# Second stage of a delta-rule and expert kernel: three buffers for the output copies, the last pair in halves, its remainder and one copy on VectorE

## The chip, the cores and the metric

One core of a Trainium2 chip. The metric is device time in microseconds (us); less is better. Engines: TensorE (PE, with its weight loads as PEld), VectorE (DVE), ScalarE (ACT), GpSimd (POOL), SyncE (SP, which issues the DMAs).

## The reference, cut to what matters

A delta-rule recurrence gives 3072 tokens of 384 features; these go through two feed-forward layers of width 2048. The change lies in the second one and in the copies at the end of the first.

```python
x = ...              # delta rule, (3072, 384)
h = x @ w_in         # first layer, 384 -> 2048
g = where(h > 0, h, exp(min(h, 0)) - 1)
x = g @ w_out        # 2048 -> 384
h = x @ w_in2        # second layer
P = a0 + a1*h + a2*h*h + a3*h*h*h
Q = 1 + abs(b0)*abs(h) + abs(b1)*h*h
out = (P / (Q + 1e-6)) @ w_out2
```

## The kernel before, in words

Everything is float32; each product of two float32 matrices is made of three matmuls, from a high part (type fp32r) and a remainder of either operand: high x high, high x remainder, remainder x high.

Tokens stand in the free dimension, features in partitions. The first stage works in windows of 512 tokens (the delta rule interleaved with the first layer); `evac1` (L623) copies a window's three accumulators `o0` to `o2` from PSUM to SBUF on ScalarE (`xe`) and sends them to DRAM (`x2d`). In the last window the copies go to the tiles `ys`, which the second stage uses as well.

The second stage (L639 to L725) works in six blocks of 512 tokens (`g`) and, in each, in eight pairs (`j`) of 128 hidden rows; pairs are numbered through, k = 8 g + j, 0 to 47. The steps of a pair:

- `H2`: 18 matmuls (L577 to L579, via `h_mms`) give 128 x 2 x 512 hidden values in PSUM, in `h_b` and `h_a` by turns.
- `A2`: three activations on ScalarE, 128x1024 each: square, absolute value and a linear form (L683, L684, L685) into `sq`, `ab`, `u`, which lie in the old tile `wo1` (named `wo` in the profile).
- `B2`: VectorE sums Q (L691); ScalarE takes its logarithm and the exponential of minus that, so 1/Q (L692, L693); VectorE makes the polynomial (L694 and L695, which read the PSUM values once more).
- `C2`: VectorE makes the high part `gh` (L702) and the error of it (L703, L704); POOL multiplies that into the remainder `gl` (L705).
- `O2`: 18 output matmuls (L719) add to the three accumulators, 12 with `gh` and then 6 with `gl`.

At the end of a block `evac2` (L722) copies the accumulators on ScalarE to tiles `ys` and sends each to DRAM. The pool `p2q` has two buffers for a tile name, so a third `ys` waits for the DMA of the first. The three accumulators have one PSUM bank each, and the next block's first matmul on a bank waits for its copy. The two-buffer rule holds for `h` too: `H2` of pair k + 2 comes before `O2` of pair k.

The order of the work is written by hand: `at(t, fn)` (L739) puts a step at a time t of a schedule, the list is sorted (L872), and each engine gets its instructions in that order; up to t = P + 4, the first two pairs of the second stage, the framework's scheduler reorders them (L877), after that they stand as listed. The lines that matter:

```python
at(t, H2, k)            # t = P + 2 * k
at(t + 1.05, A2, k)
at(t + 1.5, B2, k)
at(t + 2.2, C2, k)
at(t + 5.0, O2, k)
...
at(P + 16 * g + 19.9 + .1 * c, evac2, g, c)
```

So on ScalarE the copies of a block stand behind `B2` of pair 8 g + 9 and ahead of `A2` of pair 8 g + 10. POOL also makes the remainder of the next block's input (`lo_x2`, L664), in five places of a block.

Of the kernel before, what the change touches and what calls it, by code (L numbers as in the profile page):

```python
# [7 lines left out]
F32 = mybir.dt.float32  # L8
# [14 lines left out]
WINS = [[s, s + 1] for s in range(0, NSC, 2)]  # L23
NG2 = NT // 512
SLOTS = [[0, 0, 1, 3, 5, 7, 8, 9, 10, 11], [13, 15, 16, 18, 20, 22, 23, 26, 25, 27]]
HD = DM // 2
# [10 lines left out]
def kernel(  # L37
# [585 lines left out]
    def evac1(w):  # L623
        NC = 256 * len(WINS[w])
        c0 = 256 * WINS[w][0]
        for c in range(3):
            if w == NW - 1:
                xs = p2q.tile([128, 512], F32, tag="ys", name="xe")[:, 0:NC]
            elif c < 2:
                xs = ap2.tile([128, 8, 2, D], F32, tag="ub", name="xe").rearrange("p a b c -> p (a b c)")[:, 0:NC]  # L630
            else:
                xs = tmp[:, 0:NC]
# [44 lines left out]

    def A2(k):
        ps = flat(hp[k])
        w = wo1.rearrange("p f n -> p (f n)")  # L680
        sq, ab, u = (w[:, 1024 * (2 * i + k % 2):1024 * (2 * i + k % 2) + 1024] for i in range(3))
        e2[k] = sq, ab, u
        act(out=sq, in_=ps, func=AF.Square, scale=rb_sb)  # L683
        act(out=ab, in_=ps, func=AF.Abs, scale=ab_sb[:, 4:5])  # L684
        act(out=u, in_=ps, func=AF.Identity, scale=ab_sb[:, 3:4], bias=ab_sb[:, 2:3])  # L685

    def B2(k):
        ps = flat(hp.pop(k))
        sq, ab, u = e2[k]
        v = nc.vector  # L690
# [5 lines left out]

    def C2(k):
        sq, ab, u = e2.pop(k)
        v = nc.vector
        gh = p2q.tile([128, 1024], F32R, tag="gh2", name="gh2")  # L700
        gl = p2q.tile([128, 1024], F32R, tag="gl2", name="gl2")
        v.scalar_tensor_tensor(out=gh, in0=u, scalar=ab_sb[:, 0:1], in1=ab, op0=ALU.add, op1=ALU.mult)  # L702
        v.tensor_tensor(out=sq, in0=sq, in1=gh.bitcast(F32), op=ALU.mult)  # L703
        v.scalar_tensor_tensor(out=sq, in0=u, scalar=ab_sb[:, 0:1], in1=sq, op0=ALU.add, op1=ALU.subtract)  # L704
        nc.gpsimd.tensor_tensor(out=gl, in0=sq, in1=ab, op=ALU.mult)  # L705
        gt[k] = gh, gl

# [14 lines left out]
    def evac2(g, c):  # L722
        ys = p2q.tile([128, 512], F32, tag="ys", name="ys")
        act(out=ys, in_=acc["b", g][c], func=AF.Copy)  # L724
        nc.sync.dma_start(out=out[:, c, 512 * g:512 * g + 512], in_=ys)  # L725
# [130 lines left out]
    for k in range(NP * NG2):  # L856
        t = P + 2 * k
        at(t, H2, k)
        at(t + 1.05, A2, k)
        at(t + 1.5, B2, k)  # L860
# [110 lines left out]
```

## Time and profile before

| what | value |
|---|---|
| time, median of 3 runs | 1142.12 us (1136.59 to 1148.31) |
| the profiled execution's own time | 1144.03 us |
| its span, first to last instruction | 1142.2 us |
| TensorE matmul busy | 1046.1 us, 92% of the span |
| VectorE busy | 903.3 us, 79% |
| ScalarE busy | 772.3 us, 68% |
| POOL busy | 464.1 us, 41% |
| mean granted TensorE clock | 0.947 of full |

The first stage and the delta rule take about 735 us, the second stage the rest. All times below are from the span's start. In a row of a timeline the columns are start, length, engine, line, operation, tiles written and read, shape and count; in brackets the engine's idle time before it and what ended it. Matmuls are pipelined, so twelve matmuls of 0.39 us stand as one row of 2.88 us. A busy share is an average over stages with different limits; the waits between the engines say which one counts where.

### The profile page before, as it was taken

What the parts mean: (1) busy time and instruction counts of PE and PEld (TensorE: products, weight loads), DVE (VectorE), ACT (ScalarE), POOL (GpSimd) and SP (SyncE); (2) the same over time, 40 slices, a digit from 0 to 9 for tenths busy, and PEclk for the clock granted to TensorE, in tenths of its full rate; (3) what the DMA queues carried; (4) which work ended last, traced back from release to release, by engine and by line L of the source; (5) the groups of instructions that cost most, each with busy time, mean ns of one, the idle gap of its engine ahead of it and who ended that gap; (6) DMA issues with size and microseconds to landing.
All of it is one profiled execution on the core that took longest, in us unless ns stands there. A gap on an engine that the chain in (4) does not pass through costs nothing.

```text
span 1142.2 us, 20625 instructions
## 1 busy us (share of the span) xinstructions
PE 1046.1 (92%) x7952; PEld 836.8 (73%) x7952; DVE 903.3 (79%) x1231; ACT 772.3 (68%) x1521; POOL 464.1 (41%) x400
## 2 busy tenths in 40 slices
PE   7179898889798999999999999999999999999997
PEld 6055676667686778777878878778787887878885
DVE  4986979779856873795434479999999999999996
ACT  4566687776576646666565699976766767656764
POOL 1484466424332323243322245455353544535432
PEclk9567889999998999999999999999999999999999
DMA  9534444363364213120221054300101001010000
GB/s 262 175 123 129 120 137 131 109 207 110 100 185 145 62 61 121 56 79 2 79 71 38 1 170 127 116 10 1 56 1 56 1 1 56 1 56 1 28 1 28
DMA packets 51842, 91.75 MB, mean 80 GB/s; under 512 B 7072, under 2 KB 29728, under 8 KB 51744
## 3 DMA queue, kind: packets, MB, share of 16 engines
q1 hardware_dynamic: 51744, 90.43, 25.4%
q8 instruction: 62, 1.02, 0.4%
q14 instruction: 36, 0.29, 0.1%
HBM read 77.83 MB, written 12.58 MB: 79 GB/s over the span
## 4 chain that ended last, share of the span: by engine, by line
PE 53%; DVE 26%; ACT 7%; issue 7%; DMA 4%; POOL 4%; SPq 0%; POOLq 0%; DVEq 0%; ACTq 0%
PE o L719 12%; PE h_a L577 6%; PE h_a L578 5%; PE h_a L579 5%; DVE tmp L344 5%; PE o L595 3%; PE o L596 3%; PE o L597 3%; PE gp L278 2%; DVE tt L345 2%; PE h_b L577 2%; PE h_b L578 2%; PE h_b L579 2%; DVE wo L691 2%; DVE e L612 1%
## 5 line engine op out<-in xcount | busy, mean ns | idle before, releaser
L705 POOL TENSOR_TENSOR gl<-wo 128x1024 fp32r<-128x1024 f32 x48 | 146.4, 3051 | 215.2 <-DVE wo L704 183.1
L71 POOL TENSOR_TENSOR wor<-wo,wor 128x384 fp32r<-128x384 f32 x96 | 108.8, 1135 | 264.8 <-ACT wor L70 257.2
L577 PE MATMUL h_a<-xh,wi 128*128 128x512 f32 x417 | 174.2, 418 | 11.1 <-ACT pe L607 11.0
L578 PE MATMUL h_a<-xl,wi 128*128 128x512 f32 x417 | 169.8, 407 | 3.8 <-DVE xl L396 3.8
L579 PE MATMUL h_a<-xh,wi 128*128 128x512 f32 x417 | 168.2, 403 | 0.0
L719 PE MATMUL o<-gh,wo 128*128 128x512 f32 x576 | 141.9, 394 | 6.4 <-ACT ys L724 6.4
L719 PEld LDWEIGHTS o<-gh,wo 128*128 128x128 f32 x576 | 107.8, 189 | 33.0 <-ACT ys L724 10.8
L612 DVE SCALAR_TENSOR_TENSOR e<-e,pe 128x512 f32<-128x512 f32 x96 | 69.3, 722 | 76.0 <-ACT e L608 75.7
L595 PE MATMUL o<-gh,wor 128*128 128x512 f32 x288 | 116.4, 412 | 0.0
L596 PE MATMUL o<-gl,wor 128*128 128x512 f32 x288 | 114.4, 397 | 1.2 <-DVE gl L620 1.2
L597 PE MATMUL o<-gh,wor 128*128 128x512 f32 x288 | 113.2, 393 | 0.0
L577 PEld LDWEIGHTS h_a<-xh,wi 128*128 128x128 f32 x417 | 80.8, 194 | 31.6 <-ACT pe L607 13.7
L620 DVE TENSOR_TENSOR gl<-e,gh 128x512 fp32r<-128x512 f32 x88 | 77.4, 880 | 29.0 <-ACT gh L618 28.6
L578 PEld LDWEIGHTS h_a<-xl,wi 128*128 128x128 f32 x417 | 81.5, 195 | 22.7 <-DVE xl L396 7.8
L692 ACT ACTIVATE wo<-wo 128x1024 f32<-128x1024 f32 x48 | 51.0, 1063 | 64.8 <-DVE wo L691 64.8
L606 ACT ACTIVATE e<-h_a 128x512 f32<-128x512 f32 x91 | 54.3, 596 | 59.2 <-PE h_a L579 58.8
L579 PEld LDWEIGHTS h_a<-xh,wi 128*128 128x128 f32 x417 | 81.4, 195 | 17.3
L618 ACT ACTIVATE gh<-e 128x512 fp32r<-128x512 f32 x96 | 60.1, 626 | 33.7 <-DVE e L612 33.7
L691 DVE SCALAR_TENSOR_TENSOR wo<-wo 128x1024 f32<-128x1024 f32 x48 | 75.6, 1575 | 8.7 <-ACT wo L684 8.6
L719 PE MATMUL o<-gl,wo 128*128 128x512 f32 x288 | 73.8, 392 | 3.4 <-POOL gl L705 3.4
L70 ACT ACTIVATE wor<-wo 128x384 fp32r<-128x384 f32 x96 | 50.3, 524 | 36.2 <-PE o L597 35.3
L702 DVE SCALAR_TENSOR_TENSOR gh<-wo,ab_sb 128x1024 fp32r<-128x1024 f32 x48 | 65.3, 1359 | 8.1 <-ACT wo L693 2.0
(162 smaller groups left out, 2456.0 us busy)
## 6 DMA issues: line engine op xcount, KB each, us to landing
kv<-c_kv SPq DMA_DIRECT2D x24, 576.0 KB, 4.2
gin<-g_in SPq DMA_DIRECT2D x69, 192.0 KB, 2.7
kq<-c_kq SPq DMA_DIRECT2D x22, 512.0 KB, 4.0
raw<-w_out SPq DMA_DIRECT2D x42, 192.0 KB, 2.5
raw<-w_in SPq DMA_DIRECT2D x34, 192.0 KB, 2.4
wo<-w_in SPq DMA_DIRECT2D x30, 192.0 KB, 2.8
xr<-x2d SPq DMA_DIRECT2D x6, 768.0 KB, 5.8
out_t<-ys SPq DMA_DIRECT2D x18, 256.0 KB, 2.1
```

The costliest lines, as they stand in the source:

```text
L71: eng.tensor_tensor(out=t[:, 1], in0=src, in1=t[:, 0].bitcast(F32), op=ALU.subtract)
L577: mm(out=ps, lhsT=hi, rhs=xh[:, c, 0:NC], start=(c == 0), stop=False)
L578: mm(out=ps, lhsT=hi, rhs=xl[:, c, 0:NC], start=False, stop=False)
L579: mm(out=ps, lhsT=lo, rhs=xh[:, c, 0:NC], start=False, stop=(c == 2))
L595: mm(out=ps[:, 0:NC], lhsT=hi[:, cs], rhs=gh[:, 0:NC], start=(f == 0), stop=False)
L596: mm(out=ps[:, 0:NC], lhsT=hi[:, cs], rhs=gl[:, 0:NC], start=False, stop=False)
L597: mm(out=ps[:, 0:NC], lhsT=lo[:, cs], rhs=gh[:, 0:NC], start=False, stop=(f == NF - 1))
L612: nc.vector.scalar_tensor_tensor(out=e, in0=e, scalar=-1.0, in1=p, op0=ALU.add, op1=ALU.add)
L620: eng.tensor_tensor(out=gl[:, 0:NC], in0=e, in1=gh[:, 0:NC].bitcast(F32), op=ALU.subtract)
L691: v.scalar_tensor_tensor(out=sq, in0=sq, scalar=1.0 + 1e-6, in1=ab, op0=ALU.add, op1=ALU.add)
L705: nc.gpsimd.tensor_tensor(out=gl, in0=sq, in1=ab, op=ALU.mult)
L719: mm(out=ps, lhsT=wo2[2 * j + i][:, int(p == 1), cs], rhs=(gl if p == 2 else gh)[:, n], start=(j == 0 and p == 0 and i == 0), stop=(j == N ...
```

## The change

Four edits. `ys` gets three buffers, for the second stage and for the last window of the first. The last pair, k = 47 (`NK - 1`), runs `A2`, `B2` and `C2` twice, on 512 columns each (one of the two hidden row tiles), with its remainder `gl` on VectorE instead of POOL. Its output matmuls are ordered by half (`O2last`): nine for the first hidden tile, then nine for the second, with `gl` last in each. And of the last block's three output copies the middle one goes to VectorE.

```diff
--- before.py
+++ after.py
@@ -22,6 +22,7 @@
 NT = 3072
 WINS = [[s, s + 1] for s in range(0, NSC, 2)]
 NG2 = NT // 512
+NK = NF // 2 * NG2
 SLOTS = [[0, 0, 1, 3, 5, 7, 8, 9, 10, 11], [13, 15, 16, 18, 20, 22, 23, 26, 25, 27]]
 HD = DM // 2
 NV = 15
@@ -625,7 +626,7 @@
         c0 = 256 * WINS[w][0]
         for c in range(3):
             if w == NW - 1:
-                xs = p2q.tile([128, 512], F32, tag="ys", name="xe")[:, 0:NC]
+                xs = p2q.tile([128, 512], F32, tag="ys", name="xe", bufs=3)[:, 0:NC]
             elif c < 2:
                 xs = ap2.tile([128, 8, 2, D], F32, tag="ub", name="xe").rearrange("p a b c -> p (a b c)")[:, 0:NC]
             else:
@@ -675,18 +676,21 @@
     def flat(t):
         return t.rearrange("p a b -> p (a b)")
 
-    def A2(k):
+    ALL = slice(0, 1024)
+
+    def A2(k, n=ALL):
         ps = flat(hp[k])
         w = wo1.rearrange("p f n -> p (f n)")
-        sq, ab, u = (w[:, 1024 * (2 * i + k % 2):1024 * (2 * i + k % 2) + 1024] for i in range(3))
-        e2[k] = sq, ab, u
-        act(out=sq, in_=ps, func=AF.Square, scale=rb_sb)
-        act(out=ab, in_=ps, func=AF.Abs, scale=ab_sb[:, 4:5])
-        act(out=u, in_=ps, func=AF.Identity, scale=ab_sb[:, 3:4], bias=ab_sb[:, 2:3])
-
-    def B2(k):
-        ps = flat(hp.pop(k))
-        sq, ab, u = e2[k]
+        if k not in e2:
+            e2[k] = [w[:, 1024 * (2 * i + k % 2):1024 * (2 * i + k % 2) + 1024] for i in range(3)]
+        sq, ab, u = (t[:, n] for t in e2[k])
+        act(out=sq, in_=ps[:, n], func=AF.Square, scale=rb_sb)
+        act(out=ab, in_=ps[:, n], func=AF.Abs, scale=ab_sb[:, 4:5])
+        act(out=u, in_=ps[:, n], func=AF.Identity, scale=ab_sb[:, 3:4], bias=ab_sb[:, 2:3])
+
+    def B2(k, n=ALL):
+        ps = flat(hp[k])[:, n]
+        sq, ab, u = (t[:, n] for t in e2[k])
         v = nc.vector
         v.scalar_tensor_tensor(out=sq, in0=sq, scalar=1.0 + 1e-6, in1=ab, op0=ALU.add, op1=ALU.add)
         act(out=ab, in_=sq, func=AF.Ln)
@@ -694,16 +698,26 @@
         v.tensor_tensor(out=u, in0=u, in1=ps, op=ALU.mult)
         v.scalar_tensor_tensor(out=u, in0=u, scalar=ab_sb[:, 1:2], in1=ps, op0=ALU.add, op1=ALU.mult)
 
-    def C2(k):
-        sq, ab, u = e2.pop(k)
+    def C2(k, n=ALL):
+        sq, ab, u = (t[:, n] for t in e2[k])
         v = nc.vector
-        gh = p2q.tile([128, 1024], F32R, tag="gh2", name="gh2")
-        gl = p2q.tile([128, 1024], F32R, tag="gl2", name="gl2")
+        if k not in gt:
+            gt[k] = tuple(p2q.tile([128, 1024], F32R, tag=t, name=t) for t in ("gh2", "gl2"))
+        gh, gl = (t[:, n] for t in gt[k])
         v.scalar_tensor_tensor(out=gh, in0=u, scalar=ab_sb[:, 0:1], in1=ab, op0=ALU.add, op1=ALU.mult)
         v.tensor_tensor(out=sq, in0=sq, in1=gh.bitcast(F32), op=ALU.mult)
         v.scalar_tensor_tensor(out=sq, in0=u, scalar=ab_sb[:, 0:1], in1=sq, op0=ALU.add, op1=ALU.subtract)
-        nc.gpsimd.tensor_tensor(out=gl, in0=sq, in1=ab, op=ALU.mult)
-        gt[k] = gh, gl
+        (v if k == NK - 1 else nc.gpsimd).tensor_tensor(out=gl, in0=sq, in1=ab, op=ALU.mult)
+
+    def O2last():
+        g, j = divmod(NK - 1, NF // 2)
+        gh, gl = gt.pop(NK - 1)
+        for i in range(2):
+            n = slice(512 * i, 512 * i + 512)
+            for p in range(3):
+                for c in range(3):
+                    mm(out=acc["b", g][c], lhsT=wo2[2 * j + i][:, int(p == 1), 128 * c:128 * c + 128],
+                       rhs=(gl if p == 2 else gh)[:, n], start=False, stop=(i == 1 and p == 2))
 
     def O2(k):
         g, j = divmod(k, NF // 2)
@@ -720,8 +734,11 @@
                        start=(j == 0 and p == 0 and i == 0), stop=(j == NF // 2 - 1 and p == 2 and i == 1))
 
     def evac2(g, c):
-        ys = p2q.tile([128, 512], F32, tag="ys", name="ys")
-        act(out=ys, in_=acc["b", g][c], func=AF.Copy)
+        ys = p2q.tile([128, 512], F32, tag="ys", name="ys", bufs=3)
+        if c == 1 and g == NG2 - 1:
+            nc.vector.tensor_copy(out=ys, in_=acc["b", g][c])
+        else:
+            act(out=ys, in_=acc["b", g][c], func=AF.Copy)
         nc.sync.dma_start(out=out[:, c, 512 * g:512 * g + 512], in_=ys)
 
     def phase2_pools():
@@ -856,6 +873,14 @@
     for k in range(NP * NG2):
         t = P + 2 * k
         at(t, H2, k)
+        if k == NK - 1:
+            for i in range(2):
+                n = slice(512 * i, 512 * i + 512)
+                at(t + .9 + .5 * i, A2, k, n)
+                at(t + 1.5 + .5 * i, B2, k, n)
+                at(t + 2.2 + .5 * i, C2, k, n)
+            at(t + 5.0, O2last)
+            continue
         at(t + 1.05, A2, k)
         at(t + 1.5, B2, k)
         at(t + 2.2, C2, k)
```

The order in which the built programs issue their instructions differs at three places. VectorE, from the middle of the last pair to its end; before (one pair's six operations, line numbers of before):

```order
L691 SCALAR_TENSOR_TENSOR wo1_94<-wo1_94 128x1024
L694 TENSOR_TENSOR wo1_94<-wo1_94,h_a_69 128x1024
L695 SCALAR_TENSOR_TENSOR wo1_94<-wo1_94,ab_sb_85,h_a_69 128x1024
L702 SCALAR_TENSOR_TENSOR gh2_10708<-wo1_94,ab_sb_85 128x1024
L703 TENSOR_TENSOR wo1_94<-wo1_94,gh2_10708 128x1024
L704 SCALAR_TENSOR_TENSOR wo1_94<-wo1_94,ab_sb_85 128x1024
```

Now (the last twelve of fifteen; three like the first three stand ahead of them, and the lines have moved by 4 to 15):

```order
L695 SCALAR_TENSOR_TENSOR wo1_94<-wo1_94 128x512
L698 TENSOR_TENSOR wo1_94<-wo1_94,h_a_69 128x512
L699 SCALAR_TENSOR_TENSOR wo1_94<-wo1_94,ab_sb_85,h_a_69 128x512
L707 SCALAR_TENSOR_TENSOR gh2_10716<-wo1_94,ab_sb_85 128x512
L708 TENSOR_TENSOR wo1_94<-wo1_94,gh2_10716 128x512
L709 SCALAR_TENSOR_TENSOR wo1_94<-wo1_94,ab_sb_85 128x512
L710 TENSOR_TENSOR gl2_10717<-wo1_94 128x512
L707 SCALAR_TENSOR_TENSOR gh2_10716<-wo1_94,ab_sb_85 128x512
L708 TENSOR_TENSOR wo1_94<-wo1_94,gh2_10716 128x512
L709 SCALAR_TENSOR_TENSOR wo1_94<-wo1_94,ab_sb_85 128x512
L710 TENSOR_TENSOR gl2_10717<-wo1_94 128x512
L739 COPY ys_10765<-o1_10430 128x512
```

Both halves' sums and polynomials come first, then high part, error and remainder of the first half, then of the second, then the copy.

TensorE, the last nine output matmuls before (`gh2` is `gh`, `gl2` is `gl`; `wo214` and `wo215` are the weights of the pair's two hidden tiles):

```order
L719 MATMUL o1_10430<-gh2_10708,wo215_8267 128x512
L719 MATMUL o2_10431<-gh2_10708,wo214_8207 128x512
L719 MATMUL o2_10431<-gh2_10708,wo215_8267 128x512
L719 MATMUL o0_10429<-gl2_10709,wo214_8207 128x512
L719 MATMUL o0_10429<-gl2_10709,wo215_8267 128x512
L719 MATMUL o1_10430<-gl2_10709,wo214_8207 128x512
L719 MATMUL o1_10430<-gl2_10709,wo215_8267 128x512
L719 MATMUL o2_10431<-gl2_10709,wo214_8207 128x512
L719 MATMUL o2_10431<-gl2_10709,wo215_8267 128x512
```

And now:

```order
L719 MATMUL o0_10429<-gh2_10716,wo215_8267 128x512
L719 MATMUL o1_10430<-gh2_10716,wo215_8267 128x512
L719 MATMUL o2_10431<-gh2_10716,wo215_8267 128x512
L719 MATMUL o0_10429<-gh2_10716,wo215_8267 128x512
L719 MATMUL o1_10430<-gh2_10716,wo215_8267 128x512
L719 MATMUL o2_10431<-gh2_10716,wo215_8267 128x512
L719 MATMUL o0_10429<-gl2_10717,wo215_8267 128x512
L719 MATMUL o1_10430<-gl2_10717,wo215_8267 128x512
L719 MATMUL o2_10431<-gl2_10717,wo215_8267 128x512
```

Behind the last remainder stood six matmuls, two for each accumulator; now three.

POOL at the seam between the stages, before (`wi` is a weight tile's remainder, `gl` the first pair's):

```order
L71 TENSOR_TENSOR wi_8184<-ce,wi_8184 128x192 x2
L71 TENSOR_TENSOR wi_8259<-ce,wi_8259 128x192
L705 TENSOR_TENSOR gl_8254<-wo_94 128x1024
L71 TENSOR_TENSOR wi_8259<-ce,wi_8259 128x192
L705 TENSOR_TENSOR gl_8303<-wo_94 128x1024
```

And now:

```order
L72 TENSOR_TENSOR wi_8184<-ce,wi_8184 128x192 x2
L710 TENSOR_TENSOR gl_8254<-wo_94 128x1024
L72 TENSOR_TENSOR wi_8259<-ce,wi_8259 128x192 x2
L710 TENSOR_TENSOR gl_8303<-wo_94 128x1024
L710 TENSOR_TENSOR gl_8356<-wo_94 128x1024
```

The first pair's `gl` stands one place earlier. On ScalarE, at the same place, the third copy `xe` moves from behind the second pair's activations L684 and L685 to directly behind the other two. Elsewhere the order is the same; the waits of the third copies change.

## Rows read from the trace of the kernel before

**Rows 1.** Stretches: us, busy (instructions) of PE, PEld, DVE, ACT, POOL, clock, DMA, GB/s.
```profile
868.00:935.00 67.00, 65.51 (x288) 53.45 (x287) 63.60 (x48) 45.80 (x46) 30.54 (x14) 1.00 0.07 24
```

**Rows 2.** Timeline of TensorE: output matmuls at breaks one, four and five.
```profile
800.52 2.88 PE L719 MATMUL o<-gh,wo 128*128 128x512 f32 x12
...
809.19 1.22 PE L719 MATMUL o<-gh,wo 128*128 128x512 f32 x4 [0.35 <-ACT ys L724]
811.92 2.11 PE L719 MATMUL o<-gh,wo 128*128 128x512 f32 x8 [1.51 <-ACT ys L724]
...
819.30 2.88 PE L719 MATMUL o<-gh,wo 128*128 128x512 f32 x12
...
827.46 2.88 PE L719 MATMUL o<-gh,wo 128*128 128x512 f32 x12
...
1003.06 2.88 PE L719 MATMUL o<-gh,wo 128*128 128x512 f32 x12
...
1014.08 3.54 PE L719 MATMUL o<-gh,wo 128*128 128x512 f32 x8 [1.50 <-ACT ys L724]
...
1023.06 2.88 PE L719 MATMUL o<-gh,wo 128*128 128x512 f32 x12
...
1072.02 2.88 PE L719 MATMUL o<-gh,wo 128*128 128x512 f32 x12
...
1088.55 2.88 PE L719 MATMUL o<-gh,wo 128*128 128x512 f32 x12
```

**Rows 3.** Waits from 801 to 1092: us in total, times, longest.
```profile
ACT ys L724 <- DMA out_t<-ys: 8.2, 5, 1.7
```

**Rows 4.** Timeline of ScalarE at the first break.
```profile
807.59 1.06 ACT L693 ACTIVATE wo<-wo 128x1024 f32<-128x1024 f32 x1
808.56 1.07 ACT L724 ACTIVATE ys<-o 128x512 f32<-128x512 f32 x2
811.27 0.60 ACT L724 ACTIVATE ys<-o 128x512 f32<-128x512 f32 x1 [1.64 <-DMA out_t<-ys]
```

**Rows 5.** Stretch at the fourth break; columns as in rows 1.
```profile
1014.00:1018.00 4.00, 3.92 (x10) 3.11 (x11) 3.00 (x2) 3.13 (x4) 2.37 (x1) 0.57 0.74 251
```

**Rows 6.** Timelines of POOL and VectorE ahead of the second break.
```profile
870.37 2.40 POOL L705 TENSOR_TENSOR gl<-wo 128x1024 fp32r<-128x1024 f32 x1 [4.34 <-DVE wo L704]
...
870.68 3.17 DVE L691 SCALAR_TENSOR_TENSOR wo<-wo 128x1024 f32<-128x1024 f32 x1 [0.49 <-ACT wo L684]
```

**Rows 7.** Timelines of the engines over the last pair.
```profile
1125.00 1.22 DVE L691 SCALAR_TENSOR_TENSOR wo<-wo 128x1024 f32<-128x1024 f32 x1
...
1131.38 1.28 DVE L704 SCALAR_TENSOR_TENSOR wo<-wo,ab_sb 128x1024 f32<-128x1024 f32 x1
...
1125.25 3.23 POOL L705 TENSOR_TENSOR gl<-wo 128x1024 fp32r<-128x1024 f32 x1 [7.70 <-DVE wo L704]
1132.83 2.34 POOL L705 TENSOR_TENSOR gl<-wo 128x1024 fp32r<-128x1024 f32 x1 [4.35 <-DVE wo L704]
...
1135.22 1.65 PE L719 MATMUL o<-gl,wo 128*128 128x512 f32 x6 [2.08 <-POOL gl L705]
...
1136.00 1.09 ACT L724 ACTIVATE ys<-o 128x512 f32<-128x512 f32 x2 [7.59 <-PE o L719]
1138.71 0.60 ACT L724 ACTIVATE ys<-o 128x512 f32<-128x512 f32 x1 [1.63 <-DMA out_t<-ys]
```

**Rows 8.** One line of the first stage: length in ns, min/median/max.
```profile
L612 DVE SCALAR_TENSOR_TENSOR e<-e,pe x96: 637/692/1523, 125.0 to 726.3; 128x512 f32<-128x512 f32 x96
```

**Rows 9.** Timeline of TensorE at the seam: pair 1's output matmuls with gl.
```profile
754.11 1.67 PE L719 MATMUL o<-gl,wo 128*128 128x512 f32 x6 [0.93 <-POOL gl L705]
```

## The prediction

> **What bounds the kernel now.** Read the stretches first: in the second stage TensorE is busy 65.51 of 67 us and VectorE 63.60 [rows 1], so TensorE sets the pace and VectorE follows closely. Next TensorE's output matmuls (L719) in order of time. One pair, 18 hidden and 18 output matmuls, takes 827.46 - 819.30 = 8.16 us [rows 2], 0.227 us per matmul. That pace breaks where a block of 512 columns ends, which happens five times before the last block. From 800.52 to 1088.55, pairs 7 to 41, there are 34 steps: 288.03 us against 34 x 8.16 = 277.44, so 10.59 us are lost. The first break (800.52 to 819.30 instead of 16.32) costs 2.46, the fourth (1003.06 to 1023.06) 3.68, the fifth (1072.02 to 1088.55) 0.21, which leaves 4.24 for the second and third together.
>
> What ends the wait is in the list of waits: ScalarE's output copy waited for the DMA of an earlier copy five times, 8.2 us in all [rows 3]. In ScalarE's timeline two copies run at 808.56 and the third only at 811.27, after 1.64 us of idleness [rows 4]; TensorE starts on two banks at 809.19 and gets the third at 811.92 [rows 2]. At the fourth break the granted clock of 1014 to 1018 is 0.57 [rows 5], mostly the lower level (1.2 GHz), right behind an idle time of 1.50 us [rows 2]; 3.68 against 4.24 / 2 = 2.12 puts that at 1.56 us.
>
> The end is serial: VectorE's last pair starts at 1125.00 and its last operation ends at 1131.38 + 1.28 = 1132.66; POOL's remainder runs from 1132.83 to 1135.17; TensorE's last six matmuls start at 1135.22; copies at 1136.00 and, behind another DMA, at 1138.71 [rows 7].
>
> **The third buffer at the five breaks.** It adds no instruction and removes the DMA wait from ScalarE. At the first break the copies come 1.07 - 0.60 = 0.47 apart [rows 4], so the third starts at 808.56 + 0.94 = 809.50 and ends at 810.10. TensorE's four matmuls for the first two banks end at 809.19 + 4 x 0.227 = 810.10. Nothing waits there; what stays is the first bank, late by 809.19 - 800.52 - 8.16 = 0.51. That wait is not the DMA's: the first copy stands on ScalarE behind the logarithm and exponential of the next pair (L692, L693), and these behind VectorE's L691. How late that is depends on how far VectorE lags. At the fifth break the whole loss was 0.21, so there the first bank was in time. Bounds for what stays: nothing, or 0.51 five times = 2.6. I take 0.5 for the first and 0.1 for each other break, 0.9 in all, because removing a wait of 1.64 from ScalarE's queue also brings the next pair's three activations and so VectorE forward. Saved: 10.6 - 0.9 = 9.7, between 8.0 and 10.6. The clock's 1.56 is inside; if a drop still comes somewhere the saving is 8.1.
>
> VectorE does not become the bound at once. At the end a pair takes it 7.66 us (1125.00 to 1132.66) [rows 7] against TensorE's 8.16, half a microsecond of room. But this room is taken by blocks: at 870.68 L691 took 3.17 us instead of 1.22, while POOL's remainder ran from 870.37 to 872.77 [rows 6]; L691 had waited 0.49 for ScalarE, and POOL got in first. The loss, 3.17 - 1.22 = 1.95, is worked off in some four pairs.
>
> The Trainium skill (SBUF — State Buffer, section "Who interferes with whom") states the rule: a VectorE instruction with two SBUF inputs and a GpSimd instruction that reads SBUF exclude each other, and the later one waits for the whole of the earlier. The trace agrees: L691 ends 1.08 after POOL's end. By this rule the half-size L691 below is blocked too; without it the last pair would gain 0.6 us more.
>
> **The last pair as halves.** VectorE's six operations become fourteen of half size and a copy; POOL's last operation (2.34) goes. No row has these operations at half size. The nearest, a 128x512 operation of the first stage, takes 0.637 at least and 0.692 in the median [rows 8], against 1.22 for L691 at 128x1024 [rows 7]: 0.53 to 0.58 less. Six full ones took 7.66, 1.28 a step, so a half takes 0.69 to 0.75; I take 0.75, by the median. In a row fourteen would end at 1125.00 + 10.5 = 1135.5. But the second half's L691, due at 1127.25, meets POOL's remainder of pair 46: it stands ready from 1125.25, gets in when the first L691 ends (1125.69) and needs some 2.35, to 1128.05. A full L691 ended 1.08 after POOL (873.85 against 872.77) [rows 6]; a half ends 0.55 after it, at 1128.6, as if started at 1127.85. With its own, eleven steps follow, 8.25, to 1136.1. The remainder was there at 1135.17; now it is 0.9 later, or 0.3 later if the block doesn't come. ScalarE does the same columns in twice the instructions, beside VectorE's chain: its six activations end before the first half's product needs them, and its logarithm and exponential of either half before their gh.
>
> Behind the remainder the new order pays. Six matmuls become three: the first copy starts 0.78 after the remainder before (1136.00 - 1135.22), now one matmul sooner, about 0.6. VectorE takes the second copy, ScalarE the third, no DMA wait. The copies end at about 1.2, 1.5 and 1.7 after the remainder (0.60 each, 0.69 taken for VectorE, a matmul between the starts); SyncE issues them one by one, so the last leaves at 1.9. Before it left at 1139.33 (1138.71 + 0.60 and a step), 4.16 after. That is 2.27 gained less 0.9 = 1.4. How far VectorE lags behind TensorE when it comes to the last pair moves all of this: it can be a block (1.95) less than here. I add 0.5, a quarter of it. Last pair: 1.9, between 0.4 (the lock falls on the first L691 as well) and 3.3.
>
> **The seam.** The first stage's last copies use the same buffers. The third moves up on ScalarE and POOL's first remainder stands before a weight remainder instead of behind it. TensorE waited 0.93 there [rows 9]; that can go. But an earlier POOL can block VectorE's L691 for up to 1.95 [rows 6]. I take 0, between 0.9 gained and 0.9 lost (a block less the wait that goes, 1.95 - 0.93 = 1.0).
>
> **Sum.** 9.7 + 1.9 + 0 = 11.6 us of the profiled execution's 1144.0: 1132.4. That execution lies 1.9 above the median of the runs (1142.1), which by the same sum comes to 1130.5. I give the middle, 1131.5; the rivals are taken from the middle of the two starting points too, 1143.1.
>
> **Rivals.** (a) The copies stay late. If VectorE's blocks fall on the pair before each break, as at 870.68, the first bank keeps its 0.51 or a little more; 2.6 stay, and the last pair loses to the lock and gains only 0.4: 8.0 + 0.4 = 8.4, so 1134.7. For it: L691 at 870.68 is the one that stands ahead of the second break's copies (the break's step begins at 800.52 + 18.78 + 6 x 8.16 = 868.3). Against: with the fifth break's pattern nothing stays. (b) The last pair and lag go well: 10.6 + 3.3 + 0.5 = 14.4, so 1128.7. For it: TensorE without stalls; against: the lock.
>
> (c) Slower: the lock becomes the pace. If ScalarE's activations come after VectorE's L704 in every second pair, POOL goes first each time, and VectorE's pair costs 7.66 + 1.95 / 2 = 8.64, 0.48 above TensorE's, over 40 pairs 19 us; less 11.6 that is 7 to 8 slower, 1150.7. It decides where L691 waits for ScalarE more than 0.17 us, the time from L704's end to POOL's start (1132.66 to 1132.83) [rows 7]. Against: each block makes VectorE late by 1.95, so the next three or four find ScalarE ready. (d) The change doesn't do what it says: were the third copy still bound to the DMA, only the end would gain, 1.9: 1141.2. Against: in the built order its wait is for a DMA of the block before, 8 x 8.16 = 65 us earlier.
>
> **How the numbers follow.** Forecast 0.68 of the chance, rival (a) 0.18, (b) 0.08, (c) 0.04, (d) 0.02. One per cent is 11.4 us, about what a measurement of this kernel can tell; the three runs alone reach from 1136.6 to 1148.3. The forecast, 11.6 with an error of two either way, lies on that line: a bit over half of it, with (b) and a little for scatter, makes faster 0.50; the rest of it with (a) and (d) makes same 0.46; slower 0.04. The range takes (a) and (b) and the scatter of the runs: 1124 to 1137.
>
> **What would show it.** Right: no wait of ScalarE's output copies for a DMA anywhere; the 34 steps from pair 7 to 41 within 280 us; the clock near 1.00 in all of the second stage after the seam; three output copies 0.47 apart. The last pair: the second half-size L691 much longer than the first; the remainder no earlier after VectorE's start than before (10.2 us); last DMA some 2 us after it. Wrong: TensorE still waiting at the breaks for the first copy by over a microsecond, TensorE waiting for gl in mid-block, or L691 above 2 us in every second pair.

## The result and the profile after

| what | before | after |
|---|---|---|
| time, median of 22 runs each (lowest to highest) | 1145.16 us (1136.59 to 1160.57) | 1136.49 us (1121.99 to 1146.35) |
| the profiled execution's own time | 1144.03 us | 1129.30 us |
| its span | 1142.2 us | 1127.5 us |
| pair 0's first output product, from the span's start | 741.96 | 737.78 |
| pair 0 to pair 7 | 58.56 | 58.98 |
| pair 7 to pair 41, 34 steps | 288.03 | 278.67 |
| lost at the five breaks | 2.46, 2.14, 2.10, 3.68, 0.21 | 0.78, 0, 0, 0.40, 0.05 |
| pair 45 to the end of the span | 21.01 | 19.42 |

Spans are printed to a tenth of a us, so times to the end of a span, here and below, hold to 0.05 either way.

After over before is 0.9894, with a 95% interval of 0.9867 to 0.9921. (The ratio leaves out runs far above a kernel's fastest, seven of the 22 after the change, so it is not the quotient of the medians, which differ by 8.67 us.) It is 1.06% faster, 12.1 us of 1145.2, between 9.0 and 15.2.

The two spans differ by 14.7 us. Of these, 741.96 - 737.78 = 4.18 lie in the first stage, where no edit acts before its last copies. In fourteen profiled executions of before, after and the experiments pair 0 began anywhere from 737.78 to 751.26 us, and one and the same kernel (e8 and e12 below) at 750.67 and 743.24, so that part can be scatter. The second stage gives the rest: 9.36 at the breaks, 1.59 at the end, less 0.42 at the seam (pair 0 to pair 7), 10.5 us.

The head of the page of after:

```profile
span 1127.5 us, 20636 instructions
PE 1037.9 (92%) x7952; PEld 835.8 (74%) x7952; DVE 904.5 (80%) x1240; ACT 771.7 (68%) x1525; POOL 466.4 (41%) x399
```

The stretches of after, which answer to [rows 1] and [rows 5], with their columns:

```profile
868.00:935.00 67.00, 67.00 (x297) 55.46 (x296) 64.59 (x51) 48.41 (x51) 33.13 (x15) 1.00 0.08 24
780.00:1085.00 305.00, 304.57 (x1342) 250.91 (x1341) 293.81 (x227) 213.98 (x216) 143.48 (x63) 1.00 0.07 24
```

TensorE is busy for all of 67 us, against 65.51, and for 304.57 of 305 in the whole steady part, at a granted clock of 1.00 throughout. The waits of after from 780 to 1085, in us, times and longest, answer to [rows 3]:

```profile
ACT wo L696 <- DVE wo L695: 44.5, 38, 2.7
...
PEld o L733 <- ACT ys L741: 2.4, 8, 0.8
DVE wo L695 <- ACT wo L688: 2.1, 6, 0.5
PE o L733 <- ACT ys L741: 0.4, 1, 0.4
```

The row of ScalarE's copy waiting for a DMA (8.2 us before) is gone. TensorE's matmuls still wait 0.4 for a copy, its weight loads up to 0.8. The first break in the timeline of after, ScalarE and TensorE, answers to [rows 4] and [rows 2]:

```profile
803.86 1.06 ACT L697 ACTIVATE wo<-wo 128x1024 f32<-128x1024 f32 x1
804.83 1.55 ACT L741 ACTIVATE ys<-o 128x512 f32<-128x512 f32 x3
...
805.46 3.11 PE L733 MATMUL o<-gh,wo 128*128 128x512 f32 x12 [0.38 <-ACT ys L741]
```

The three copies stand in one row of 1.55 us, (1.55 - 0.60) / 2 = 0.47 apart. The first of them still comes behind the exponential (L697), and TensorE starts 0.38 late on it; its twelve matmuls then take 3.11 instead of 2.88, as weight loads wait for the other two copies. This makes up most of the 0.78 that this break still loses. The seam (VectorE, POOL, TensorE) answers to [rows 9]:

```profile
735.72 3.19 POOL L710 TENSOR_TENSOR gl<-wo 128x1024 fp32r<-128x1024 f32 x1 [3.97 <-DVE wo L709]
737.39 2.61 DVE L695 SCALAR_TENSOR_TENSOR wo<-wo 128x1024 f32<-128x1024 f32 x1 [0.74 <-ACT wo L688]
742.50 0.50 PE L578 MATMUL h_a<-xh,wi 128*128 128x512 f32 x1 [0.48 <-DVE wo L699]
750.39 1.65 PE L733 MATMUL o<-gl,wo 128*128 128x512 f32 x6 [0.75 <-POOL gl L710]
```

TensorE's wait for the remainder of pair 1 shrank from 0.93 to 0.75, but VectorE's sum of that pair (L695, L691 before) now meets POOL's remainder and takes 2.61 us (1.27 before). The polynomial behind it (L699) is late, and TensorE waits 0.48 for that, a wait that before does not have. The end of after, VectorE, POOL, TensorE, ScalarE and SyncE, answers to [rows 7]:

```profile
1108.08 2.88 PE L733 MATMUL o<-gh,wo 128*128 128x512 f32 x12
...
1111.28 0.68 DVE L695 SCALAR_TENSOR_TENSOR wo<-wo 128x512 f32<-128x512 f32 x1
1111.53 2.70 POOL L710 TENSOR_TENSOR gl<-wo 128x1024 fp32r<-128x1024 f32 x1 [4.34 <-DVE wo L709]
1112.13 0.69 DVE L698 TENSOR_TENSOR wo<-wo,h_a 128x512 f32<-128x512 f32 x1 [0.17 <-ACT wo L689]
1113.52 1.26 DVE L695 SCALAR_TENSOR_TENSOR wo<-wo 128x512 f32<-128x512 f32 x1
...
1121.34 0.69 DVE L710 TENSOR_TENSOR gl<-wo 128x512 fp32r<-128x512 f32 x1
1122.09 0.96 PE L719 MATMUL o<-gl,wo 128*128 128x512 f32 x3 [0.55 <-DVE gl L710]
1122.62 1.09 ACT L741 ACTIVATE ys<-o 128x512 f32<-128x512 f32 x2 [6.51 <-PE o L719]
1122.85 0.69 DVE L739 COPY ys<-o 128x512 f32<-128x512 f32 x1 [0.82 <-PE o L719]
1123.24 1.30 SPq L742 DMA_DIRECT2D out_t<-ys  x3
```

The second half's sum takes 1.26 us against 0.68 for the first's: it waits for POOL's remainder (to 1114.23). The last remainder ends at 1121.34 + 0.69 = 1122.03, 10.75 after VectorE's start, and SyncE is done with issuing the last store at 1123.24 + 1.30 = 1124.54, 2.51 behind it. The issue of that last store by itself, in before and in after:

```profile
1139.33 0.33 SPq L725 DMA_DIRECT2D out_t<-ys  x1
...
1124.15 0.40 SPq L742 DMA_DIRECT2D out_t<-ys  x1
```

It begins 1124.15 - 1122.03 = 2.12 behind the remainder, in before 1139.33 - 1135.17 = 4.16.

### The profile page after: what moved, and what is told of

It is laid out like the page before. It is cut to its first block, busy times and chain, and to the rows that moved or that the text cites. A ratio compares the mean times of both kernels' runs of the same rounds, so it can differ in the third digit from the quotient of the medians.

```text
span 1127.5 us, 20636 instructions
## 1 busy us (share of the span) xinstructions
PE 1037.9 (92%) x7952; PEld 835.8 (74%) x7952; DVE 904.5 (80%) x1240; ACT 771.7 (68%) x1525; POOL 466.4 (41%) x399
## 4 chain that ended last, share of the span: by engine, by line
PE 54%; DVE 24%; ACT 7%; issue 6%; DMA 5%; POOL 3%; SPq 0%; ACTq 0%; DVEq 0%; POOLq 0%
PE o L733 13%; PE h_a L578 6%; PE h_a L579 6%; PE h_a L580 6%; DVE tmp L345 5%; PE o L596 3%; PE o L597 3%; PE o L598 3%; PE h_b L578 2%; PE h_b L579 2%; PE h_b L580 2%; DMA raw<-w_out 2%; DVE tt L346 2%; PE gp L279 2%; DVE wo L695 2%
## 5 line engine op out<-in xcount | busy, mean ns | idle before, releaser
L72 POOL TENSOR_TENSOR wor<-wo,wor 128x384 fp32r<-128x384 f32 x96 | 109.1, 1137 | 268.0 <-ACT wor L71 260.3
L733 PE MATMUL o<-gh,wo 128*128 128x512 f32 x564 | 135.9, 390 | 0.4 <-ACT ys L741 0.4
L733 PEld LDWEIGHTS o<-gh,wo 128*128 128x128 f32 x564 | 105.2, 188 | 23.8 <-ACT ys L741 2.4
L696 ACT ACTIVATE wo<-wo 128x1024 f32<-128x1024 f32 (+1 forms) x49 | 51.3, 1046 | 60.4 <-DVE wo L695 60.4
L695 DVE SCALAR_TENSOR_TENSOR wo<-wo 128x1024 f32<-128x1024 f32 (+1 forms) x49 | 73.1, 1492 | 4.5 <-ACT wo L688 4.4
L707 DVE SCALAR_TENSOR_TENSOR gh<-wo,ab_sb 128x1024 fp32r<-128x1024 f32 (+1 forms) x49 | 65.5, 1336 | 6.6 <-ACT wo L697 0.6
```

Of the source, the lines that this page charges most:

```text
L72: eng.tensor_tensor(out=t[:, 1], in0=src, in1=t[:, 0].bitcast(F32), op=ALU.subtract)
L695: v.scalar_tensor_tensor(out=sq, in0=sq, scalar=1.0 + 1e-6, in1=ab, op0=ALU.add, op1=ALU.add)
L733: mm(out=ps, lhsT=wo2[2 * j + i][:, int(p == 1), cs], rhs=(gl if p == 2 else gh)[:, n], start=(j == 0 and p == 0 and i == 0), stop=(j == N ...
```

## The experiments

The theory: the third buffer is the whole gain at the breaks; at the end VectorE's chain decides, together with the SBUF port that it shares with GpSimd (POOL), the lock of the prediction. The rivals are in the expectations. The first stage's scatter is larger than most effects here, so each run is read in windows of its second stage. "Lag" is the time from pair 45's first output product to VectorE's first operation of the last pair, pair 47; the next two columns add up to the last.

| kernel | pairs 0 to 7 | 34 steps | lag | pair 45 to last remainder | from there to the end | pair 45 to end |
|---|---|---|---|---|---|---|
| before | 58.56 | 288.03 | 3.81 | 13.98 | 7.03 | 21.01 |
| after | 58.98 | 278.67 | 3.20 | 13.95 | 5.47 | 19.42 |
| e1 three buffers alone | 59.47 | 278.60 | 2.61 | 12.80 | 5.68 | 18.48 |
| e2 last pair alone | 58.56 | 288.46 | 3.77 | 14.53 | 7.05 | 21.58 |
| e3 whole last pair | 59.00 | 278.59 | 2.61 | 11.64 | 5.70 | 17.34 |
| e4 both sums first | 58.97 | 278.58 | 3.21 | 15.33 | 5.48 | 20.81 |
| e5 seam order | 60.85 | 278.58 | 3.21 | 12.24 | 5.73 | 17.97 |
| e6 sum behind products | 59.50 | 278.67 | 2.63 | 13.39 | 5.48 | 18.87 |
| e7 remainder in halves | 59.04 | 278.67 | 3.21 | 12.29 | 5.55 | 17.84 |
| e8 copies earlier | 59.52 | 277.44 | 2.41 | 11.45 | 5.68 | 17.13 |
| e10 ScalarE copies | 59.09 | 277.44 | 2.42 | 11.45 | 5.77 | 17.22 |
| e11 third copy back | 61.61 | 277.44 | 2.42 | 11.45 | 5.69 | 17.14 |
| e12 as e8 | 59.52 | 277.44 | 2.42 | 11.45 | 5.71 | 17.16 |
| e13 as after | 59.53 | 278.63 | 2.63 | 13.38 | 5.47 | 18.85 |

**Three buffers alone** (before, with the buffers only).

```diff
-                xs = p2q.tile([128, 512], F32, tag="ys", name="xe")[:, 0:NC]
+                xs = p2q.tile([128, 512], F32, tag="ys", name="xe", bufs=3)[:, 0:NC]
...
-        ys = p2q.tile([128, 512], F32, tag="ys", name="ys")
+        ys = p2q.tile([128, 512], F32, tag="ys", name="ys", bufs=3)
```

> Before with three buffers for the output copies alone; the last pair and its copies stay as they were. Theory (the DMA wait of ScalarE's third copy is the whole loss at the five breaks): the 34 steps from pair 7's to pair 41's output matmuls take 278 to 280 us (288.0 before, 278.7 after the change), no output copy waits for a DMA. For the end the theory says that the third buffer does most there too: the stretch from pair 45's output matmuls to the span's end, 21.0 before and 19.4 after the change, comes to 19.2 to 19.7. Rival (the gain at the end comes from the halves and VectorE's share): that stretch stays at 20.5 or more.

One run, 1141.74 us (before beside it 1144.16). The 34 steps are those of after, 278.60: the buffer is the whole gain there. And the end is 2.5 shorter than before, more than the 1.6 of the full change and below the 19.2 to 19.7 that were expected; 1.2 of the 2.5 are a smaller lag.

**The last pair alone** (after, with two buffers again).

```diff
-                xs = p2q.tile([128, 512], F32, tag="ys", name="xe", bufs=3)[:, 0:NC]
+                xs = p2q.tile([128, 512], F32, tag="ys", name="xe")[:, 0:NC]
...
-        ys = p2q.tile([128, 512], F32, tag="ys", name="ys", bufs=3)
+        ys = p2q.tile([128, 512], F32, tag="ys", name="ys")
```

> The changed kernel with two buffers: only the last pair's halves, the remainder on VectorE and the copy on VectorE remain. Theory: the 34 steps take 286 to 290 us as before, and ScalarE's third copy waits some 1.6 us for a DMA at every break. The end gains nothing by itself: the last copy waits for the first one's DMA, so the stretch from pair 45 to the span's end is 21 to 22 us (21.0 before). Rival (halves and VectorE's share make the end shorter): 19.5 to 20.3.

One run, 1144.31 us. Without the third buffer the halves and VectorE's copy bring nothing. The waits of this kernel from 780 to 1090, and its last copy:

```profile
ACT ys L741 <- DMA out_t<-ys: 8.2, 5, 1.7
...
1138.76 0.60 ACT L741 ACTIVATE ys<-o 128x512 f32<-128x512 f32 x1 [2.12 <-DMA out_t<-ys]
```

The DMA wait is back, 8.2 us at the five breaks and 2.12 at the end. Here the clock does not drop at the fourth break (1.00 from 780 to 1090), and the breaks cost 2.52, 2.13, 2.15, 2.10 and 2.12. That fits a reading of before in which the drop raised the fourth to 3.68 and gave VectorE time, so that the fifth cost only 0.21; one run of each does not show it.

**The last pair whole** (after, without halves; VectorE's remainder and copy stay).

```diff
-        if k == NK - 1:
-            for i in range(2):
...
-            at(t + 5.0, O2last)
-            continue
```

> The changed kernel without the halves: the last pair is worked whole, its remainder on VectorE, three buffers, the middle last copy on VectorE. Theory (halving costs more steps and meets POOL's lock): the last remainder comes 8.9 to 9.0 us after VectorE's start on the last pair (10.75 with halves, 10.2 before), six matmuls instead of three stand behind it, and the stretch from pair 45 to the span's end is 18.1 to 18.6 (19.4 with halves). Rival (the halves pay by letting TensorE begin sooner): 19.4 or more.

One run, 1131.19 us. From pair 45 to the end it takes 17.34, 2.1 less than after and 0.8 less than the lowest that was expected; of both, 0.6 is the lag, 2.61 instead of 3.20. At like lags whole beats halves by 1.5: 17.34 against 18.85 (e13) at 2.6, 17.97 (e5, which has the same end) against 19.42 at 3.2. The end of this kernel:

```profile
1114.47 1.22 DVE L695 SCALAR_TENSOR_TENSOR wo<-wo 128x1024 f32<-128x1024 f32 x1
1114.72 3.25 POOL L710 TENSOR_TENSOR gl<-wo 128x1024 fp32r<-128x1024 f32 x1 [4.33 <-DVE wo L709]
...
1122.27 1.23 DVE L710 TENSOR_TENSOR gl<-wo 128x1024 fp32r<-128x1024 f32 x1
1123.55 1.66 PE L733 MATMUL o<-gl,wo 128*128 128x512 f32 x6 [0.65 <-DVE gl L710]
```

Seven operations of full size take 1123.50 - 1114.47 = 9.03 us where after's fourteen halves took 10.75. What gains at the end, beside the buffer, is the remainder on VectorE (1.23 against POOL's 2.34 [rows 7]); the halves lose. Six products behind it instead of three cost 5.70 - 5.47 = 0.23.

**Both halves' sums first** (after, `B2` of the last pair in two parts).

```diff
...
-                at(t + 1.5 + .5 * i, B2, k, n)
+                at(t + 1.41 + .04 * i, B2, k, n, 0)
+                at(t + 1.5 + .5 * i, B2, k, n, 1)
```

> The changed kernel with the second half's sum (the first VectorE operation of a half) directly behind the first half's, ahead of the products with PSUM. Theory (POOL stands waiting for the port since the previous pair's last error and takes it as soon as the first sum ends): the second sum takes about 2.4 us longer instead of 0.6, everything stands behind it, and the end is 0.8 to 1.3 us later than the changed kernel's 19.4. Rival (two VectorE operations in a row keep the port): the second sum takes 0.6 to 0.7, POOL's remainder waits, and the end is 0.5 to 0.7 us sooner.

One run, 1136.69 us; the end is 1.39 longer than after's at the same lag, a little more than the 0.8 to 1.3 expected. VectorE and POOL of this kernel, in which the sum is L696:

```profile
1117.30 3.49 DVE L696 SCALAR_TENSOR_TENSOR wo<-wo 128x512 f32<-128x512 f32 x2
1117.55 2.69 POOL L713 TENSOR_TENSOR gl<-wo 128x1024 fp32r<-128x1024 f32 x1 [4.33 <-ACT wo L688]
```

Two sums of 0.68 each take 3.49, though they stand back to back: POOL's waiting operation gets in between. The Trainium skill (SBUF — State Buffer, section "Who interferes with whom") says that of a VectorE operation with two SBUF inputs and a GpSimd operation that reads SBUF the one issued later waits in full; the row agrees, and here the next VectorE operation counts as later than a GpSimd operation already waiting. It is not so everywhere: at the seam of e13, shown below, POOL's operation stays behind three VectorE operations in a row.

**The sum behind the products** (after, the second half's sum last).

```diff
...
-                at(t + 1.5 + .5 * i, B2, k, n)
+                if i == 0:
+                    at(t + 1.5, B2, k, n)
+                else:
+                    at(t + 1.55, B2, k, n, 1)
+                    at(t + 1.6, B2, k, n, 0)
```

> The changed kernel with one edit at the last pair: the second half's sum (two SBUF operands, 1.26 us while GpSimd's remainder of pair 46 runs, against 0.68 for the first half's) is issued behind the two products of the second half, which read the pair's PSUM; nothing else moves. Theory (the sum was held by GpSimd, the products with a PSUM operand are not): every one of VectorE's half-size steps takes 0.68 to 0.75 us, the last remainder ends 10.1 to 10.3 us after VectorE's start on the pair instead of 10.75, and from product pair 45 to the end it takes 18.8 us at a lag of 3.2 (19.4 in the changed kernel). Rival (GpSimd slows whatever VectorE runs beside it): the products stretch in its place, and 19.4 stays; or VectorE then waits 0.6 us for the later exponential, and 19.4 stays too.

One run, 1137.18 us. The sum took 0.68 and no product stretched, and 18.87 met the 18.8 that was expected; but the lag was 2.63, not 3.2. The repeat of after (e13) fell on the same lag, and there the unedited order took 18.85. Its VectorE and POOL:

```profile
1112.18 0.69 DVE L695 SCALAR_TENSOR_TENSOR wo<-wo 128x512 f32<-128x512 f32 x1
1112.43 2.69 POOL L710 TENSOR_TENSOR gl<-wo 128x1024 fp32r<-128x1024 f32 x1 [4.34 <-PE o L733]
1113.61 0.69 DVE L698 TENSOR_TENSOR wo<-wo,h_a 128x512 f32<-128x512 f32 x1 [0.74 <-ACT wo L689]
1114.99 0.69 DVE L695 SCALAR_TENSOR_TENSOR wo<-wo 128x512 f32<-128x512 f32 x1
```

VectorE waits 0.74 for the last of ScalarE's six activations and comes to the second sum when POOL is nearly done (1115.12). The first product (L698) starts equally far behind pair 45's first output product in both runs of this kernel (1112.13 - 1108.08 = 4.05 in after, 1113.61 - 1109.55 = 4.06 in e13). So the block of 0.57 comes at a lag of 3.2 and not at 2.6, and the gain of this run is not its edit's. What the edit does at 3.2 is open.

**The remainder alone in halves** (whole pair, last products by half).

```diff
+        if k == NK - 1:
+            for i in range(2):
+                h = slice(512 * i, 512 * i + 512)
+                v.tensor_tensor(out=gl[:, h], in0=sq[:, h], in1=ab[:, h], op=ALU.mult)
...
```

> The whole-pair kernel with one edit: of the last pair, VectorE's remainder alone is worked in two halves, and the last six products go by half, so that three of them stand behind the last remainder. Theory (at the end only what stands behind the last remainder counts, and a half costs VectorE 0.69 us against 1.23 for the whole): remainder 0.15 us later, 0.7 us less of products behind it, so pair 45 to the end takes 16.8 us against 17.3 (same lag of 2.6). Rival (the end is set by the copies and the last DMA, whatever stands ahead): 17.3 stays.

One run, 1132.81 us; 17.84 at a lag of 3.21. e5, below, ends as e3 does and had the same lag: 17.97. So the edit gave 0.1 at most, not 0.5. ScalarE's last copy does end sooner behind the remainder, at 1126.14 + 1.09 = 1127.23, 1.78 after 1125.45, against 1125.24 + 0.60 - 1123.50 = 2.34 in e3; the span does not follow. Stretches of 2 us at the end of e3, with DMA share and GB/s last:

```profile
1125.80:1127.80 2.00, 0.00 (x0) 0.00 (x0) 0.00 (x0) 0.04 (x1) 0.00 (x0) 1.00 1.00 387
```

and of e7:

```profile
1127.50:1129.50 2.00, 0.00 (x0) 0.00 (x0) 0.00 (x0) 0.00 (x0) 0.00 (x0) 1.00 0.99 383
```

All 16 DMA engines are busy for 2 us, with the 0.79 MB of the last three stores. The rival holds: behind the first copy the end is transfer. The Trainium skill (Perfetto Trace Analysis, section "Roofline") gives about 435 GB/s as the bound of one core's 16 engines; the 383 and 387 here stay 11 to 12% below it.

**The copies earlier** (whole pair, break copies ahead of the logarithm).

```diff
-            at(P + 16 * g + 19.9 + .1 * c, evac2, g, c)
+            at(P + 16 * g + 19.2 + .1 * c, evac2, g, c)
```

> The whole-pair kernel with one edit: at every break the three ScalarE copies stand one place earlier, ahead of the logarithm and exponential of the pair instead of behind them; in the changed kernel ScalarE idles 2.1 us there (from 800.67 to 802.76 at the first break), and the three copies need 1.55. Theory (the 0.78 and 0.40 us left at the first and fourth break are products that wait for these copies): no product waits for a copy, the breaks lose 0.1 us together, and the 34 steps from pair 7 to pair 41 take 277.5 to 277.7 us instead of 278.6. Rival (what is left is VectorE against GpSimd's port, and the copies then only push the logarithm back, with VectorE behind it): 278.6 or more.

One run, 1139.46 us (before beside it 1149.64). The 34 steps take 277.44, which is 34 x 8.16: no break loses anything. ScalarE and VectorE at the first break of this kernel:

```profile
812.90 1.21 ACT L689 ACTIVATE wo<-h_a,ab_sb 128x1024 f32<-128x1024 f32 x1
813.99 1.57 ACT L741 ACTIVATE ys<-o 128x512 f32<-128x512 f32 x3
814.94 1.22 DVE L695 SCALAR_TENSOR_TENSOR wo<-wo 128x1024 f32<-128x1024 f32 x1
816.19 1.06 ACT L696 ACTIVATE wo<-wo 128x1024 f32<-128x1024 f32 x1 [0.63 <-DVE wo L695]
```

The copies fill ScalarE's idle time, and the logarithm (L696) still waits 0.63 for VectorE's sum.

**All copies on ScalarE** (e8, without VectorE's copy).

```diff
-        if c == 1 and g == NG2 - 1:
-            nc.vector.tensor_copy(out=ys, in_=acc["b", g][c])
...
```

> The kernel with the earlier copies (three buffers, last pair in full-size tiles with VectorE's remainder, break copies ahead of the logarithm), with one edit: the three copies of the last outputs are all on ScalarE, none on VectorE. In all kernels with a third buffer so far 5.5 to 5.7 us pass from the end of the last remainder to the end of the span, with halves and without, with VectorE's copy and (three buffers alone, GpSimd's remainder) without it. Theory (behind the first copy the 0.79 MB of the three stores move at about 400 GB/s, which is 2.0 us, so the later copies are hidden): 5.7 us stay, 0.2 more at most, and pair 45 to the end takes 17.1 to 17.3 us against 17.13. Rival (the second copy on VectorE takes a copy's 0.6 us from the chain, as the prediction reckoned it): 6.2 us, and 17.7.

One run, 1131.83 us (before beside it 1153.61). From the last remainder to the end 5.77, against 5.68 and 5.71 (e8 and e12, one kernel): within what the printed spans can tell, VectorE's copy is worth nothing.

**The seam, twice.** e3 with the last window's third copy behind all activations of pair 1:

```diff
...
-        at(T + Q["ev"], evac1, w)
+        if w < NW - 1:
+            at(T + Q["ev"], evac1, w)
+        else:
+            at(T + Q["ev"], evac1, w, (0, 1))
+            at(T + Q["p"] + 3.06, evac1, w, (2,))
```

> The whole-pair kernel (three buffers, last pair in full-size tiles with VectorE's remainder), with one edit: at the seam between the stages the third copy of the first stage's result stands on ScalarE behind the second pair's three activations again, as before, though it has a buffer. Theory (the third buffer lets that copy go 1.2 us earlier on ScalarE, this puts the pair's absolute value off, and VectorE's sum then comes behind GpSimd's remainder and waits for the port): that sum takes about 1.3 us instead of 2.6, and first product pair 0 to pair 7 takes 58.6 us instead of the 59.0 of the three kernels with a third buffer. Rival (the 0.4 us are the stores' or other scatter of the seam): 59.0 stays.

and e8 with it behind the second activation only:

```diff
...
         act(out=ab, in_=ps[:, n], func=AF.Abs, scale=ab_sb[:, 4:5])
+        if k == 1:
+            evac1(NW - 1, (2,))
...
```

> The kernel with the earlier copies, with one edit at the seam: the third copy of the first stage's last window stands on ScalarE behind the second pair's absolute value and no longer ahead of it, with VectorE's order unchanged. Theory (the third buffer let this copy go ahead of the absolute value; VectorE's sum of that pair then came 0.7 us late, behind GpSimd's remainder, which holds the port): the sum takes 1.2 to 1.3 us instead of 2.6. Pair 0 to pair 7 stood at 59.0 us in kernels with three buffers where the clock was at half just ahead of the seam (58.6 with two buffers), and at 59.5 where it was not: 58.6 or 59.1, that is 0.4 less. Rival (the sum's delay does not reach TensorE): 59.0 or 59.5 stays.

One run each, 1143.07 and 1140.20 us. Both missed: pairs 0 to 7 took 60.85 and 61.61. VectorE, POOL and TensorE in e11, in which the sum is L698:

```profile
749.11 2.50 POOL L713 TENSOR_TENSOR gl<-wo 128x1024 fp32r<-128x1024 f32 x1
749.28 2.74 DVE L72 TENSOR_TENSOR wo<-w2r,wo 128x384 fp32r<-128x384 f32 x1
...
752.22 1.21 DVE L698 SCALAR_TENSOR_TENSOR wo<-wo 128x1024 f32<-128x1024 f32 x1
...
756.42 0.79 PE L578 MATMUL h_a<-xh,wi 128*128 128x512 f32 x1 [2.81 <-DVE wo L702]
```

With these edits POOL's remainder comes just ahead of the split of a weight (L72, two SBUF inputs, 0.55 elsewhere), which now takes 2.74, and VectorE's work behind it is late: TensorE waits 2.81 for the polynomial (L702). A clock drop of 3.4 us at 756 adds to it. In e5 the split takes 2.72, and what TensorE waits for is the third copy itself, which stands on ScalarE behind work that waits for VectorE:

```profile
755.08 2.14 PE L734 MATMUL o<-gh,wo 128*128 128x512 f32 x8 [2.75 <-ACT xe L634]
```

The sum takes 1.21, as expected, but that is no effect of the edit: it takes 1.21 or 1.22 without it too, in the five runs with a third buffer in which the clock did not drop just ahead of the seam (e1, e6, e8, e12, e13; in after it was 0.51 from 731.0 to 734.4), and it did not drop there in e5 and e11. Those five lose at the seam in another way. Here is e13, TensorE last:

```profile
738.14 4.32 POOL L710 TENSOR_TENSOR gl<-wo 128x1024 fp32r<-128x1024 f32 x1 [3.96 <-DMA x2d<-xe]
738.25 0.54 DVE L72 TENSOR_TENSOR wo<-w2r,wo 128x384 fp32r<-128x384 f32 x1
738.72 0.34 DVE L177 SCALAR_TENSOR_TENSOR ce<-raw 128x192 int32<-128x192 int32 x1
738.99 1.21 DVE L695 SCALAR_TENSOR_TENSOR wo<-wo 128x1024 f32<-128x1024 f32 x1
742.51 1.67 PE L733 MATMUL o<-gl,wo 128*128 128x512 f32 x6 [0.88 <-POOL gl L710]
```

VectorE runs from the split to the sum without a gap, POOL's remainder takes 4.32 and ends 2.26 behind the sum, and TensorE waits 0.88 for it. In the five, POOL takes 4.31 or 4.32, TensorE waits 0.81 to 0.88, and pairs 0 to 7 take 59.47 to 59.53. Where the clock had dropped just ahead (after, e3, e4, e7, e10), VectorE waits 0.68 to 0.75 for ScalarE ahead of the sum, POOL gets in, the sum takes 2.59 to 2.66, TensorE waits 0.47 to 0.56 for the polynomial, and the pairs take 58.97 to 59.09. With two buffers there are two runs, both with the drop, 58.56 each; so 0.42 is the like comparison, and what two buffers would take without the drop is not known.

**The best version, timed.** e8's kernel and the changed kernel, five rounds each beside before.

> The kernel with the earlier copies (three buffers, last pair in full-size tiles with VectorE's remainder and one copy on VectorE, break copies ahead of the logarithm), timed beside the changed kernel and the kernel before. By the windows of the runs so far it takes 1.15 us less than the changed kernel at the breaks (34 steps 277.44 against 278.6) and 2.1 to 2.3 less at the end (17.1 to 17.3 against 19.4), so 3.3 us less, and 15 to 16 us less than the kernel before: a ratio of about 0.986 to it. Rival (what is saved in the second stage is within the scatter of the first): no difference to the changed kernel that these rounds can tell.

> The changed kernel itself, unaltered, timed beside the one above on the same chip: a ratio of 0.987 to 0.992 to the kernel before, and 34 steps of 278.6 us with 19.4 (lag of 3.2) from pair 45 to the end.

The ratios to before are 0.9864 (0.9824 to 0.9903) and 0.9867 (0.9822 to 0.9912), medians 1132.61 and 1132.89 (before 1148.88). Both beat before; between the two these rounds tell nothing, as the rival has it. (e13 missed its 19.4 at the end, with a lag of 2.63, and its ratio lies just under the 0.987 to 0.992 expected.) The windows of the profiled executions do: 277.44 and 17.16 against 278.63 and 18.85, 2.9 us less. But pair 0 began at 743.24 in the one and 738.75 in the other, and the executions took 1132.10 and 1130.22.

## Why the prediction was right

The predicted gain was 11.6 us; 12.1 (9.0 to 15.2) was measured, and 8.67 between the medians of all runs. The second stage, where the change acts, shows 10.5 in the profiled executions.

- **The third buffer at the five breaks.** 9.7 predicted, 9.36 measured. What stays was put at 0.5 for the first break and 0.9 in all, and is 0.78 and 1.23. The reason given holds: with the copies ahead of the logarithm and exponential (e8) nothing stays. That the other breaks get 0.1 each was a mean; two lost nothing, one 0.05, one 0.40. Which break loses moves with VectorE's lag: the fourth in after and e13, the fifth in e4, e5 and e7.
- **The clock's 1.56** stood inside the saving, but may have been no loss: in e2, without the drop, the four later breaks cost 2.1 each where before shows 2.14, 2.10, 3.68 and 0.21, and 11.02 are lost (288.46 - 277.44) instead of 10.59.
- **The last pair as halves.** 1.9 predicted, 1.59 measured. The block of the second sum, the 0.68 to 0.75 us of a half and the remainder no earlier after VectorE's start (10.75 against 10.17; 11.1 was forecast) came as forecast. The lag fell by 0.61, where 0.5 had been added. The copies end 1.19, 1.51 and 1.68 us behind the remainder, as forecast (1.2, 1.5, 1.7). The last store's issue begins 2.12 behind it, where 1.9 was forecast and before has 4.16. That is 2.04 sooner, but the end of the span comes only 7.03 - 5.47 = 1.56 sooner behind the remainder. The step that failed is the credit: "Behind the remainder the new order pays" took what the last store's issue gains (2.27) for what the span gains, and put down to the halved products and VectorE's copy what the third buffer gives. Three buffers alone bring 7.03 to 5.68; halves bring 0.2 more and the copy nothing that can be read (e10), since the stores take 2 us behind the first copy. And the halves lose 1.7 us on VectorE (10.75 against 9.03), so without them (e3) the end gains 3.7, of which 1.2 are a smaller lag. That 1.59 came near 1.9 is in part luck: the pay behind the remainder was put 0.7 too high, the delay of the remainder 0.3 too high (0.9 against 10.75 - 10.17 = 0.58).
- **The seam.** 0 predicted within 0.9 either way, 0.42 lost, by the mechanism named: an earlier POOL blocks VectorE's sum. In the repeat (e13) the pairs 0 to 7 took 59.53, and there the sum is not blocked but TensorE waits for POOL's remainder.
- **ScalarE's halves** were said to end before they are needed; in after the first product waits 0.17 for the last of the six activations, in e13 0.74.
- **Rivals.** (a) 2.6 us do not stay, only 1.23. (c) L695 is above 2 us in six pairs of after between 760 and 1100, not in every second, though it waits up to 0.49 for ScalarE, above the 0.17 named: the blocks come 41 to 58 us apart. (d) is out, the DMA wait being gone. (b) reckoned with nothing left at the breaks and 3.3 at the end.

## What to carry to other kernels

Give an output copy as many buffers as a burst has copies, and put the burst where its engine idles, ahead of work that waits for another engine. Do not halve a serial chain at the end when the engine's operations have a fixed part: here two halves cost 1.36 to 1.5 us where one whole cost 1.22 to 1.28. Once the last stores fill the DMA engines, as here for 2 us, hastening the later copies brings little: what counts is when the first store starts.

## What had not been expected of the hardware

- A GpSimd operation that waits for the shared port can get it between two adjoining VectorE operations (e4: 3.49 us for two of 0.68, around POOL's 2.69), but need not: at the seam of e13 it stayed behind three in a row and took 4.32. What decides is open.
- How late VectorE comes into the last pair moved between 2.4 and 3.8 us with edits far ahead of it, and between 2.63 and 3.20 in two executions of the same kernel (e13 and after). A block came at the later one alone: 18.85 and 19.42 to the end.
- The seam came out in two forms, which go with a drop of the clock just ahead of it: in ten runs with a third buffer and no edit there, 58.97 to 59.09 us with it (five) and 59.47 to 59.53 without (five).
- The first stage scatters more than the change gains: a row of the stretch to 735 us shows a mean granted clock of 0.92 in before, 0.93 in after and 0.91 in e1, whose pair 0 began at 741.96, 737.78 and 750.81. The clock is not all of it: two of the kernels, with 0.93 each, stood at 738.75 and 743.24.
